# Loading a group of attention values in one transfer and sorting them with 0/1 matmuls

## The chip, the cores and the metric

The kernel runs on one core of one Trainium2 chip. The metric is the time on the device in microseconds (us), of which the median of several runs is given. A profile is one further execution, recorded by the hardware; its times count from the start of its span.

## What is computed

The reference has two parts. The first is attention over 4 batches, 8 heads, 768 positions and a head dimension of 64. Heads 0, 2 and 6 ("retrieval" heads) see every earlier key. The other five ("streaming" heads) see only the last 64 keys and the first 4 keys, the sinks.

```
scores = where(mask, q @ k.T / sqrt(64), -1e9)
a = softmax(scores)            # mask: causal for heads 0, 2, 6;
attn = a @ v                   # causal & (key < 4 | query - key < 64) for the others
x = attn as (3072, 512)
out = sum over e of p[:, e] * (relu(x @ w1[e]) @ w2[e])
```

The second part is a mixture of four dense experts over all 3072 rows: p is the normalised `domain_probs`, w1[e] is 512 x 1024 and w2[e] is 1024 x 512.

## The kernel before

The 3072 rows are worked on in eight groups of 384 rows (half of one batch each). Group g needs one attention (`attention(b, c)`) and then four expert units (`moe_steps`, one per expert). The first group's attention runs alone, at the start; the attention of group g + 1 is woven into the expert units of group g by a planner in the main loop, which counts the nanoseconds of matmuls issued. The order of the instructions of every engine is written out by hand (`manual_schedule`), and each engine executes its own list in order.

Everything that matters here happens in the first 45 us.

*Loads by SyncE and ScalarE (lines 350 to 372).* The q and k rows of group 0 come in as fp32, one load per head, with a small load `v_s32` of the four sink rows of v (line 353) between them, and then `probs`. The queue of SyncE is q1, that of ScalarE q10.

*GpSimd's list (lines 376 to 480).* GpSimd builds the masks and issues, on queue q0, all loads that turn fp32 into fp16: the values v and the expert weights. Its order before is: identity matrix, v of head 0, `mask_c`, `mask_s` (lines 397 to 420, three fills and three selects), v of heads 2, 1, 3, 4, 6, 5, w1 of expert 0 (line 300, two loads), v of head 7, w2 of expert 0 (line 306), zero fills, w1 of expert 1, a wait until w1 of expert 0 has landed (`landed`, line 460), k and q of group 1 in "triples" (line 212), w2 of expert 1, and so on.

*Where values go.* For a retrieval head, `vR` holds three tiles of 128 consecutive keys (line 269). For a streaming head, `vS` holds four tiles of 96 keys on partitions 32 to 127, and each tile also has the four sink rows on partitions 0 to 3. Before, line 275 loads the 96-key tiles from memory, and `sink_row` (line 283) copies the sink rows from `v_s32` with VectorE, once per streaming head.

*The first attention (lines 777 to 806).* For each pair of heads, `transposes` turns q and k (line 512, copies on ScalarE and VectorE); `scores(h)` multiplies (line 613), adds the mask by a matmul (line 625) and takes the exponential on ScalarE (line 631); `values(h)` multiplies with v (line 661 for retrieval heads, line 725 for streaming ones) and divides by the sum (line 678 on VectorE, or lines 743 to 758 on ScalarE). `warm_up` (line 388) adds matmuls on zeros at fixed places. The result `xT` feeds the expert units: the first layer is line 894, its relu line 907, the second layer line 918, the weighted sum on VectorE lines 930 and 934.

PSUM tiles come from three pools: pA (4 buffers), pV (2) and pO (2).

Of the kernel before, what the change touches and what calls it, by code (L numbers as in the profile page):

```python
# [9 lines left out]
FP32 = mybir.dt.float32  # L10
FP16 = mybir.dt.float16
AF = mybir.ActivationFunctionType
ALU = mybir.AluOpType
# [4 lines left out]
def kernel(  # L18
# [33 lines left out]
    nc = tc.nc  # L52
    P = 128
    B, H, S, D = q.shape
    E, DM, F = moe_w1.shape
    CH = 3 * P
# [13 lines left out]
    SH = [h for h in range(H) if not RETR[h]]  # L70
    NS = int(n_sink)
    NW = int(window)
    TK = 96
# [83 lines left out]
    def own_v(h):  # L157
        return half(PLACE[h][1])
# [10 lines left out]
    def v_tiles(b, c, h):  # L169

        if RETR[h]:
            return vR[b % 2][:, 3 * c : 3 * c + 3, RH.index(h), :]
        if b:
            return windows(vSf, c)[:, :, SH.index(h), :]
        return vS[:, c, :, SH.index(h), :]
# [89 lines left out]
    def load_v(b, c, heads):  # L265
        for h in heads:
            t = v_tiles(b, c, h)
            if RETR[h]:
                gp.dma_start(out=t[:, :, 0:D], in_=rows_of(v, b, h, c))  # L269
            elif b:  # L270
                gp.dma_start(  # L271
                    out=t[:, :, own_v(h)], in_=windows_of(v, b, h, c)
                )
            else:
                gp.dma_start(  # L275
                    out=t[R0:P, :, own_v(h)],
                    in_=tiles_of(v, b, h, c),
                )

    def sink_row(h):  # L280

        t = v_tiles(0, 0, h)
        nc.vector.tensor_copy(
            out=t[0:NS, :, own_v(h)],
            in_=v_s32[:, h : h + 1, :].to_broadcast([NS, TC, D]),
        )

    def sink_rows(b, c):
        if b:
            put_sinks(windows(vSf, c), v_sinks, c)  # L290
# [55 lines left out]

    q32 = moe.tile([P, 3, H, D], FP32, name="q32", tag="hs", bufs=2)
    k32 = moe.tile([P, 3, H, D], FP32, name="k32", tag="hs", bufs=2)

    v_s32 = pers.tile([NS, H, D], FP32, name="v_s32")  # L350
    for h in range(H):
        if h == 2:
            nc.sync.dma_start(
                out=v_s32, in_=v[0, :, 0:NS, :].rearrange("h r d -> r h d")
            )
        nc.sync.dma_start(out=k32[:, :, h, :], in_=rows_of(k, 0, h, 0))
        if h == HP:

            nc.scalar.add_instruction(
                mybir.InstLoadActFuncSet(  # L360
                    name=nc.get_next_instruction_name(),
                    engine=ENG.Activation,
                    act_func_set_id=[x.name for x in SETS].index(
                        "natural_log_exp_and_others"
                    ),
                )
            )
        eng = nc.scalar if h < HP else nc.sync
        eng.dma_start(out=q32[:, :, h, :], in_=rows_of(q, 0, h, 0))
# [5 lines left out]
    nc.vector.memset(ones, ONES)  # L375
    make_identity(nc, ident32)
    one_values(nc.vector, 0)
    load_v(0, 0, [0])
    zero(nc.vector, kR[0][:, 0, :, :, :])
    zero(nc.vector, kS[:, 0, :, :, :].rearrange("p t s x -> p s t x"))  # L380
    nc.vector.tensor_copy(out=ident16, in_=ident32)
# [13 lines left out]
    def mask_c(x, keep, drop):  # L395

        gp.memset(x, keep)
        for i in range(2):
            gp.affine_select(
                out=x[:, i * P : (i + 1) * P], in_=x[:, i * P : (i + 1) * P],  # L400
                compare_op=ALU.is_ge, fill=drop, base=0, pattern=[[1, P]],
                channel_multiplier=-1,
            )

    def mask_s(x, n, keep, drop):

        gp.memset(x, keep)
        gp.affine_select(
            out=x, in_=x, compare_op=ALU.is_ge, fill=drop,
            base=R0, pattern=[[0, n], [1, TQ]], channel_multiplier=-1,  # L410
        )
        gp.affine_select(  # L412
            out=x, in_=x, compare_op=ALU.is_ge, fill=drop,
            base=NW - 1 - R0, pattern=[[0, n], [-1, TQ]], channel_multiplier=1,
        )
        gp.memset(x[0:R0, :, :], drop)
        gp.memset(x[0:NS, :, 0:TK], keep)
        gp.affine_select(
            out=x[0:NS, 0, 0:TK], in_=x[0:NS, 0, 0:TK], compare_op=ALU.is_ge,
            fill=drop, base=-NW, pattern=[[1, TK]], channel_multiplier=-1,  # L420
        )

    def mask_w():
# [19 lines left out]
            base=WQ - 1 - NW, pattern=[[1, WQ]], channel_multiplier=-1,  # L443
        )

    mask_c(bC, 0.0, -60000.0)
    mask_s(bS[:, 0:2, :], 2, 0.0, -60000.0)
    load_v(0, 0, [2, 1, 3, 4, 6, 5])
    load_w1(0, 0, F)
    load_v(0, 0, [7])  # L450
    load_w2(0)
    zero(gp, kR[0][:, 1, :, :, :])
    zero(gp, kS[:, 1, :, :, :].rearrange("p t s x -> p s t x"))
# [40 lines left out]
    def attention(b, c):  # L494
# [109 lines left out]
        def scores(h):  # L604
            hp = h // 2
            es_of[h] = []
            for cols, parts, masks in score_tiles(h):
                ps = bank()
                if first and not es_of[h]:
                    warm_up(ps, {0: 5, 2: 8}.get(h, 0), P)  # L610
                ns = 0
                for n, (t, o, q0, nq) in enumerate(parts):
                    nc.tensor.matmul(  # L613
                        out=ps[:, o : o + nq],
                        lhsT=key_tile(b, c, h, t),
                        rhs=qTs[b, c][:, hp, q0 : q0 + nq],
                        start=(n == 0 or not first),
                        stop=not first,
                        skip_group_check=first,
                    )  # L620
                    ns += mm_ns(nq)
                if first:
                    for m, mo, o0, o1 in masks:
                        bias = bC if m is mC else bSf
                        nc.tensor.matmul(
                            out=ps[:, o0:o1], lhsT=ident16,
                            rhs=bias[:, mo : mo + o1 - o0],
                            start=False, stop=True, skip_group_check=True,
                        )
                es = att.tile([P, 512], FP16, name="es", bufs=12)  # L630
                nc.scalar.activation(  # L631
                    out=es[:, 0:cols], in_=ps[:, 0:cols], func=AF.Exp, scale=SC
                )
                for m, mo, o0, o1 in () if first else masks:
                    nc.vector.tensor_tensor(  # L635
                        out=es[:, o0:o1],
                        in0=es[:, o0:o1],
                        in1=m[:, mo : mo + o1 - o0],
                        op=ALU.mult,
                    )  # L640
                es_of[h].append((es, parts))
                if first:
                    tick(LAG)
                yield ns
# [63 lines left out]
        def values(h):  # L708
# [52 lines left out]

            yield ns + (600.0 if g == 1 else 0.0)

        def both(a, bb):

            gens = [a, bb]
            while gens:
                for gg in list(gens):
                    try:
                        yield next(gg)  # L770
                    except StopIteration:
                        gens.remove(gg)
# [4 lines left out]
        if first:  # L777
            yield from transposes(0)
            yield from scores(0)
            sink_row(1)  # L780
            sink_row(3)
            nc.scalar.copy(out=bS[:, 2, :], in_=bS[:, 1, :])
            yield from transposes(1)
            yield from scores(2)
            sink_row(4)
            sink_row(5)
            sink_row(7)
            yield from both(scores(1), values(0))
            yield from transposes(2)
            yield from both(scores(3), values(2))  # L790
            x_transposes(0)
            yield from scores(4)
            yield from transposes(3)
            yield from values(1)
            yield from both(scores(5), values(3))
            yield from both(scores(6), values(4))
            yield from both(scores(7), values(6))
            yield from values(5)
            x_transposes(6)
            yield from values(7)  # L800
            tick(LAG)
            small_things()
        else:
            sink_rows(b, c)
            order = (0, 2, 6, 1, 3, 5, 7, 4) if by_dma else (0, 2, 1, 3, 6, 5, 7, 4)
            if not by_dma:
                yield from transposes(0)
                yield from transposes(1)

            waiting = []  # L810
            for n, h in enumerate(order):
                v_steps = iter(())
                if len(waiting) > (0 if by_dma else 1):
                    v_steps = values(waiting.pop(0))
                yield from both(scores(h), v_steps)
                waiting.append(h)
                if not by_dma and n in (1, 3):
                    yield from transposes({1: 3, 3: 2}[n])
            for h in waiting:
                yield from values(h)  # L820
# [214 lines left out]
```

The softmax here doesn't subtract the row's maximum and nothing guards it: scores larger than these inputs give would overflow.

## Time and profile before

| | |
|---|---|
| median of 3 runs | 399.17 us (399.09 to 400.34) |
| span of the profiled execution | 398.9 us |
| TensorE busy | 389.1 us (98%) |
| VectorE, ScalarE, GpSimd busy | 156.6, 219.0, 143.6 us |
| first attention on TensorE | 4.69 to 20.62 us |
| loads of v of group 0 on GpSimd | eight, of 0.68 to 0.90 us each, at 1.50 to 12.28 us |

"Busy" is time in which the engine had an instruction running. A high share says that an engine is rarely idle, but not which stage is limited by what; for this one reads the timeline (instructions in order of time, with what ended the idle time before each) and the stage table (the busy time of every engine in a stretch, with TensorE's granted clock). For a load, the profile gives the time at which the engine issued it, the packets of each queue in a stretch, and the share of the 16 DMA engines' time that these took; packets overlap, so shares can exceed 100%.

### The profile page before, as it was taken

How to read it: one execution, taken by the hardware profiler on the slowest of the kernel's cores; microseconds unless marked ns; L12 is line 12 of the kernel's file. 1: busy time of each engine (PE TensorE's matmuls, PEld its weight loads, DVE VectorE, ACT ScalarE, POOL GpSimd, SP SyncE). 2: the span in 40 equal slices, each digit the busy share in tenths (PEclk: the TensorE clock that was granted, in tenths of full speed). 3: DMA queues.
4: the chain of work that ended last, by engine and by line, in shares of the span. 5: the costliest groups of instructions: out<-in, count | busy, mean ns of one | idle time of the engine just before them, and what ended most of it. 6: DMA issues, size and time to landing. Idle time of an engine off the chain costs nothing.

```text
span 398.9 us, 7125 instructions
## 1 busy us (share of the span) xinstructions
PE 389.1 (98%) x2823; PEld 220.5 (55%) x2823; DVE 156.6 (39%) x344; ACT 219.0 (55%) x468; POOL 143.6 (36%) x183
## 2 busy tenths in 40 slices
PE   7897999999999999999999999999999999999996
PEld 4753466555555555555555555555555555655553
DVE  7743585324342334433342233433443223432222
ACT  4754459535776546655664446845464456853331
POOL 8823795808907905920049101950000000000000
PEclk9999899999999999999999999999999999999999
DMA  9999999999999999990789949990472000020002
GB/s 170 154 202 204 185 196 157 130 197 136 111 196 148 113 127 130 127 120 3 126 104 163 74 80 135 97 168 12 76 123 80 5 12 0 12 79 2 0 2 80
DMA packets 166133, 42.23 MB, mean 106 GB/s; under 512 B 156396, under 2 KB 161108, under 8 KB 166100
## 3 DMA queue, kind: packets, MB, share of 16 engines
q0 software_dynamic: 102656, 20.98, 63.4%
q1 hardware_dynamic: 61700, 20.34, 26.7%
q10 hardware_dynamic: 1744, 0.46, 0.5%
q8 instruction: 22, 0.36, 0.4%
q14 instruction: 11, 0.09, 0.1%
HBM read 43.57 MB, written 6.29 MB: 125 GB/s over the span
## 4 chain that ended last, share of the span: by engine, by line
PE 89%; DMA 7%; POOL 3%; issue 0%; DVE 0%; DVEq 0%; POOLq 0%
PE pO L918 40%; PE pA L894 39%; PE pA L613 5%; DMA w2sb<-in_moe_w_dram 5%; DMA w1sb<-in_moe_w_dram 2%; PE pV L725 2%; PE pV L661 2%; POOL vS L275 1%; POOL vR L269 1%; POOL bS L412 0%; PE pV L862 0%; PE pA L515 0%; POOL k L212 0%; POOL q L212 0%; PE pV L515 0%
## 5 line engine op out<-in xcount | busy, mean ns | idle before, releaser
L894 PE MATMUL pA<-xT,w1sb 128*128 128x384 f16 x1024 | 185.9, 326 | 0.1
L918 PE MATMUL pO<-w2sb,hs 128*128 128x512 f16 x760 | 180.4, 381 | 2.8 <-DMA w2sb<-in_moe_w_dram 2.8
L907 ACT ACTIVATE hs<-pA 128x384 f16<-128x384 f32 x256 | 122.0, 492 | 94.9 <-PE pA L894 89.7
L894 PEld LDWEIGHTS <-w1sb 128*128 128x128 f16 x1024 | 95.9, 98 | 59.6 <-issue 0.5
L918 PEld LDWEIGHTS <-hs 128*128 128x128 f16 x760 | 71.0, 98 | 76.9 <-DMA w2sb<-in_moe_w_dram 3.1
L631 ACT ACTIVATE es<-pA 128x384 f16<-128x384 f32 (+2 forms) x122 | 60.0, 511 | 57.0 <-PE pA L613 55.9
L934 DVE SCALAR_TENSOR_TENSOR acc<-pO,p_sb,acc 128x512 f32<-128x512 f32 x71 | 53.3, 750 | 71.7 <-PE pO L918 71.3
L227 POOL DMA_DIRECT2D kSr<-in_k_dram x30 | 30.1, 1003 | 31.9 <-DMA kS<-kSr 21.8
L223 POOL DMA_DIRECT2D kRr<-in_k_dram x18 | 14.0, 777 | 70.8 <-DMA kR<-kRr 70.8
L748 DVE TENSOR_TENSOR xT<-pV,rc 64x384 f16<-64x384 f32 x37 | 20.5, 554 | 32.0 <-ACT rc L753 24.3
L271 POOL DMA_DIRECT2D vS<-in_v_dram x30 | 30.2, 1011 | 0.0
L930 DVE TENSOR_SCALAR acc<-pO,p_sb 128x512 f32<-128x512 f32 x24 | 18.0, 751 | 28.7 <-PE pO L918 28.5
L635 DVE TENSOR_TENSOR es<-es,mC 128x256 f16<-128x256 f16 (+1 forms) x42 | 10.9, 259 | 46.6 <-ACT es L631 45.6
L743 ACT ACTIVATE rc<-pV,eps 64x384 f32<-64x384 f32 x37 | 21.3, 576 | 12.0 <-PE pV L725 11.5
L613 PE MATMUL pA<-qT,kR 128*128 128x384 f16 (+2 forms) x120 | 24.4, 278 | 0.9 <-ACT qT L524 0.4
L753 ACT ACTIVATE rc<-rc 64x384 f32<-64x384 f32 x38 | 19.8, 521 | 1.2
L269 POOL DMA_DIRECT2D vR<-in_v_dram x24 | 19.0, 793 | 0.1
L635 DVE TENSOR_TENSOR es<-es,mW 128x384 f16<-128x384 f16 x30 | 10.7, 358 | 16.9 <-ACT es L631 16.8
L613 PEld LDWEIGHTS <-kR 128*128 128x128 f16 x120 | 11.4, 98 | 10.6 <-DVE kR L531 1.1
L661 PEld LDWEIGHTS <-es 128*128 128x128 f16 x252 | 13.2, 97 | 7.2 <-ACT es L631 0.9
L613 PEld LDWEIGHTS <-kS 128*128 128x128 f16 x255 | 13.3, 98 | 6.6
L725 PEld LDWEIGHTS <-vS 128*128 128x128 f16 x255 | 13.4, 98 | 5.9 <-DMA vS<-in_v_dram 0.4
(102 smaller groups left out, 187.6 us busy)
## 6 DMA issues: line engine op xcount, KB each, us to landing
out_dram<-acc SPq DMA_DIRECT2D x23, 256.0 KB
w1sb<-in_moe_w_dram POOLq DMA_DIRECT2D x8, 512.0 KB, 9.6
w2sb<-in_moe_w_dram POOLq DMA_DIRECT2D x4, 1024.0 KB, 14.8
kSr<-in_k_dram POOLq DMA_DIRECT2D x30, 112.0 KB, 3.8
vS<-in_v_dram POOLq DMA_DIRECT2D x30, 112.0 KB, 6.0
q<-in_q_dram POOLq DMA_DIRECT2D x18, 128.0 KB, 4.3
vR<-in_v_dram POOLq DMA_DIRECT2D x24, 48.0 KB, 5.3
kRr<-in_k_dram POOLq DMA_DIRECT2D x18, 48.0 KB, 4.2
```

Of the source, the lines that this page charges most:

```text
L227: gp.dma_start(out=kSr[:, :, SH.index(h), own(h)], in_=windows_of(k, b, h, c),)
L269: gp.dma_start(out=t[:, :, 0:D], in_=rows_of(v, b, h, c))
L271: gp.dma_start(out=t[:, :, own_v(h)], in_=windows_of(v, b, h, c))
L613: nc.tensor.matmul(out=ps[:, o : o + nq], lhsT=key_tile(b, c, h, t), rhs=qTs[b, c][:, hp, q0 : q0 + nq], start=(n == 0 or not first), stop ...
L631: nc.scalar.activation(out=es[:, 0:cols], in_=ps[:, 0:cols], func=AF.Exp, scale=SC)
L635: nc.vector.tensor_tensor(out=es[:, o0:o1], in0=es[:, o0:o1], in1=m[:, mo : mo + o1 - o0], op=ALU.mult,)
L725: nc.tensor.matmul(out=ps[:, q0 : q0 + nq], lhsT=v_tile(b, c, h, t), rhs=es[:, o : o + nq], start=(n == 0), stop=(n == len(work) - 1), ski ...
L743: nc.scalar.activation(out=rc[r, :], in_=ps[o, 0:CH], func=AF.Ln, bias=eps[o, :])
L894: nc.tensor.matmul(out=pss[ft][:, 0:CH], lhsT=w1sb[:, e * DMP + ct, ft * P : (ft + 1) * P], rhs=xT[g][:, ct, :], start=(n == 0), stop=(n = ...
L907: nc.scalar.activation(out=hs[:, ft, :], in_=ps[:, 0:CH], func=AF.Relu)
L918: nc.tensor.matmul(out=ps_o, lhsT=hs[:, ft, j * P : (j + 1) * P], rhs=w2sb[:, e * FTP + ft, :], start=(ft == 0), stop=(ft == FTP - 1),)
L934: nc.vector.scalar_tensor_tensor(out=acc[nt], in0=ps_o, scalar=p_ap, in1=acc[nt], op0=ALU.mult, op1=ALU.add,)
```

## The change

The eight loads of v of group 0 and the load of the sink rows go. In their place, one load (`load_triples`, as for k and q of group 1) puts three consecutive rows of each head on each partition of a tile `v16` (128 x 8 heads x 3 rows x 64, fp16). GpSimd issues it inside `mask_s`, after the second select. It also builds two 0/1 matrices, `pick_r` (128 x 386) and `pick_s` (128 x 4 x 3 x 128): a fill and one select for the first, ahead of `mask_s`; a fill and eight selects for the second, between the loads of w1 and w2 of expert 0.

Matmuls with slices of these matrices carry the rows from `v16` to the partitions that the tiles want, sinks included: 18 matmuls for the retrieval heads (`pick_values_r`, two PSUM tiles) and 12 for each of the sets (1, 3), (4, 5) and (7) (`pick_values_s`). ScalarE copies the five PSUM tiles into `vR` and `vS`. The calls stand at fixed places in the first attention; the five `sink_row` copies on VectorE go.

```diff
-    def sink_row(h):
...
-        if h == 2:
-            nc.sync.dma_start(
-                out=v_s32, in_=v[0, :, 0:NS, :].rearrange("h r d -> r h d")
-            )
...
-    load_v(0, 0, [0])
...
+        between()
         gp.memset(x[0:R0, :, :], drop)
...
+    pick_r = pers.tile([P, CH + 2], FP16, name="pick_r")
+    pick_s = pers.tile([P, TC, 3, P], FP16, name="pick_s")
+    def ones_where(x, base, pattern):
+        gp.affine_select(
+            out=x, in_=x, compare_op=ALU.not_equal, fill=1.0, base=base,
+            pattern=pattern, channel_multiplier=3,
+        )
     mask_c(bC, 0.0, -60000.0)
-    mask_s(bS[:, 0:2, :], 2, 0.0, -60000.0)
-    load_v(0, 0, [2, 1, 3, 4, 6, 5])
+    gp.memset(pick_r, 0.0)
+    ones_where(pick_r, 2, [[-1, CH + 2]])
+    v16 = att.tile([P, H, 3, D], FP16, name="q16", bufs=2)
+    mask_s(
+        bS[:, 0:2, :], 2, 0.0, -60000.0, lambda: load_triples(v, v16, 0, 0)
+    )
     load_w1(0, 0, F)
-    load_v(0, 0, [7])
+    gp.memset(pick_s, 0.0)
+    for t in range(TC):
+        ones_where(pick_s[:, t, :, R0:P], -TK * t, [[1, 3], [-1, TK]])
+        ones_where(pick_s[:, t, :, 0:NS], 0, [[1, 3], [-1, NS]])
     load_w2(0)
...
+        def pick_values_r(blocks, copy):
...
+            for n, t in enumerate(blocks):
+                for j in range(3):
+                    lhsT = pick_r[:, 2 + P * t - j : 2 + P * t - j + P]
+                    for h0, h1, rhs in (
+                        (0, 2, v16[:, 0:3:2, j, :]), (2, 3, v16[:, 6:7, j, :])
+                    ):
+                        nc.tensor.matmul(
...
+            copy(
+                out=vR[0][:, blocks[0] : blocks[-1] + 1, :, 0:D], in_=x
+            )
+        def pick_values_s(heads, step, copy):
...
+            for t in range(TC):
+                for j in range(3):
+                    nc.tensor.matmul(
+                        out=x[:, :, t, :], lhsT=pick_s[:, t, j, :],
+                        rhs=v16[:, heads[0] : heads[-1] + 1 : step, j, :],
...
             yield from scores(0)
-            sink_row(1)
-            sink_row(3)
             nc.scalar.copy(out=bS[:, 2, :], in_=bS[:, 1, :])
             yield from transposes(1)
             yield from scores(2)
-            sink_row(4)
-            sink_row(5)
-            sink_row(7)
+            pick_values_r([0, 1], nc.scalar.copy)
+            pick_values_r([2], nc.scalar.copy)
             yield from both(scores(1), values(0))
             yield from transposes(2)
+            pick_values_s((1, 3), 2, nc.scalar.copy)
             yield from both(scores(3), values(2))
             x_transposes(0)
             yield from scores(4)
             yield from transposes(3)
             yield from values(1)
+            pick_values_s((4, 5), 1, nc.scalar.copy)
             yield from both(scores(5), values(3))
+            pick_values_s((7,), 1, nc.scalar.copy)
             yield from both(scores(6), values(4))
```

More of the change, by code (lines that the diff above doesn't have):

```diff
@@ L278, in load_v @@
                 )
-    def sink_row(h):
[L282 to L285, printed above, removed]
-        )
     def sink_rows(b, c):
@@ L348 @@
     k32 = moe.tile([P, 3, H, D], FP32, name="k32", tag="hs", bufs=2)
-    v_s32 = pers.tile([NS, H, D], FP32, name="v_s32")
     for h in range(H):
-        if h == 2:
-            nc.sync.dma_start(
-                out=v_s32, in_=v[0, :, 0:NS, :].rearrange("h r d -> r h d")
-            )
         nc.sync.dma_start(out=k32[:, :, h, :], in_=rows_of(k, 0, h, 0))
@@ L403, in mask_c, with mask_s @@
             )
-    def mask_s(x, n, keep, drop):
+    def mask_s(x, n, keep, drop, between):
         gp.memset(x, keep)
@@ L762, in values @@
             yield ns + (600.0 if g == 1 else 0.0)
+        def pick_values_r(blocks, copy):
+            ps = pV.tile([P, 512], FP32, name="pV", bufs=2)
+            x = ps[:, 0 : len(blocks) * NR * D].rearrange(
+                "p (t h d) -> p t h d", t=len(blocks), h=NR
+            )
[6 more added lines that the diff above has]
+                        nc.tensor.matmul(
+                            out=x[:, n, h0:h1, :], lhsT=lhsT, rhs=rhs,
+                            start=(n == 0 and j == 0 and h0 == 0),
+                            stop=(n == len(blocks) - 1 and j == 2 and h0 == 2),
+                            skip_group_check=True,
+                        )
+            copy(
+                out=vR[0][:, blocks[0] : blocks[-1] + 1, :, 0:D], in_=x
+            )
+        def pick_values_s(heads, step, copy):
+            n = len(heads)
+            ps = pO.tile([P, 512], FP32, name="pO", bufs=2)
+            x = ps[:, 0 : n * TC * D].rearrange("p (s t d) -> p s t d", s=n, t=TC)
+            for t in range(TC):
[3 more added lines that the diff above has]
+                        rhs=v16[:, heads[0] : heads[-1] + 1 : step, j, :],
+                        start=(t == 0 and j == 0),
+                        stop=(t == TC - 1 and j == 2),
+                        skip_group_check=True,
+                    )
+            s0 = SH.index(heads[0])
+            copy(
+                out=vS[:, 0, :, s0 : s0 + n, own_v(heads[0])].rearrange(
+                    "p t s d -> p s t d"
+                ),
+                in_=x,
+            )
         def both(a, bb):
```

## The prediction

> **What bounds the kernel now.** I read the page first, then TensorE's stages, its timeline, and the timelines of ScalarE and GpSimd up to 42 us. On the page TensorE is busy in 98% of the span, but its clock digit drops once, in the fifth slice (40 to 50 us), and the DMA row is full to 180 us:
>
> ```profile
> PEclk9999899999999999999999999999999999999999
> DMA  9999999999999999990789949990472000020002
> ```
>
> TensorE's timeline shows where it stood still before that (start, us, instruction, wait before it):
>
> ```profile
> 20.62 5.76 PE L894 MATMUL pA<-xT,w1sb 128*128 128x384 f16 x32
> ...
> 36.26 1.47 PE L894 MATMUL pA<-xT,w1sb 128*128 128x384 f16 x8
> 40.49 1.04 PE L918 MATMUL pO<-w2sb,hs 128*128 128x512 f16 x4 [2.75 <-DMA w2sb<-in_moe_w_dram]
> ```
>
> The expert layers start at 20.62. The second expert's w2 is needed at 37.74 and starts work at 40.49: 2.75 us lost to a transfer. The stage table (length, then each engine's busy us, clock, DMA share, GB/s) shows the second half of that price:
>
> ```profile
> 37.74:40.49 2.75, 0.00 (x0) 0.00 (x1) 0.33 (x1) 0.69 (x2) 1.25 (x2) 1.00 1.20 213
> 40.49:41.58 1.09, 1.09 (x8) 0.43 (x10) 0.00 (x0) 0.00 (x0) 0.70 (x2) 1.00 1.09 205
> 41.58:45.00 3.42, 3.42 (x19) 1.39 (x18) 2.99 (x4) 0.00 (x0) 2.44 (x4) 0.51 1.47 188
> ```
>
> After the idle stretch TensorE runs 3.42 us at half clock, so another 1.7 us are lost. From 40.5 to 385 us it is busy in every stage to the last hundredth and waits for nothing. So the end is set by TensorE alone: whatever moves its work after 40.5 us moves the end by as much. What counts is (a) when the first attention ends, now 20.62, and (b) whether the 2.75 + 1.7 = 4.45 us remain.
>
> In the first attention TensorE and ScalarE hand work to each other:
>
> ```profile
> 9.14 0.30 PE L613 MATMUL pA<-qT,kS 128*128 128x160 f16 x2
> 9.42 0.35 PE L661 MATMUL pV<-vR,es 128*128 128x65 f16 x6
> 10.54 0.30 PE L613 MATMUL pA<-qT,kS 128*128 128x160 f16 x2
> 17.81 0.30 PE L661 MATMUL pV<-vR,es 128*128 128x65 f16 x4 [0.77 <-ACT es L631]
> ```
>
> ```profile
> 11.01 0.79 ACT L631 ACTIVATE es<-pA 128x320 f16<-128x320 f32 x2 [0.36 <-PE pA L625]
> 12.11 0.71 ACT L631 ACTIVATE es<-pA 128x320 f16<-128x320 f32 x2 [0.31 <-PE pA L625]
> 13.24 0.58 ACT L743 ACTIVATE rc<-pV,eps 64x384 f32<-64x384 f32 x1 [0.41 <-PE pV L725]
> 18.36 0.38 ACT L631 ACTIVATE es<-pA 128x256 f16<-128x256 f32 x1 [0.28 <-PE pA L625]
> ```
>
> To 13.24 us ScalarE waits for TensorE (0.36, 0.31, 0.41); from there to 18.1 it has no gap, and TensorE waits for it (0.77). The attention's slack is small, and the change puts work on both.
>
> **What the Trainium skill says.** "TensorE: Matmul & The Clock Gate", Part 1: the clock falls to half after an idle window and comes back after a busy one; windows run freely, 3413 ns each. The trace agrees: half clock lasts 3.42 us, and a window with 1.09 us of work in 3.41 was enough to lose it. "DMA: Bandwidth & Descriptors", "Why small descriptors are slow": each packet carries a fixed overhead. The trace agrees: alone between 7 and 8 us, q1 moved 833 packets of 256 bytes, and between 32 and 33 us q0 moved 505 packets of the three-row kind (768 bytes read):
>
> ```profile
> q1 hardware_dynamic: 833, 0.20, 112.6%
> q0 software_dynamic: 505, 0.19, 160.0%
> ```
>
> That is 19.2 and 31.7 ns of one of 16 engines. The same page, "Queues, rings and completion order": an engine serves its queues in turn, a packet at a time. The trace agrees roughly: from 8 to 9 us q1 got 511 and q0 323 packets.
>
> **Transfers.** Removed: eight loads (3072 packets, 3072 x 19.2 / 16 = 3.7 us of all engines); added: one of 1024 (x 31.7 / 16 = 2.0 us). The weights behind it gain some 1.6 us. Dropping the small sink load on SP (0.43 us of issue) lets later q and k loads start earlier; TensorE waited for none of them (no gap at 6.85), so 0.
>
> **GpSimd.** The rows that place the load:
>
> ```profile
> 1.50 0.90 POOL L269 DMA_DIRECT2D vR<-in_v_dram  x1
> 4.27 1.44 POOL L412 TENSOR_SCALAR_AFFINE_SELECT bS<-bS 128x320 f16<-128x320 f16 x1
> 6.72 0.78 POOL L269 DMA_DIRECT2D vR<-in_v_dram  x1
> 20.31 0.90 POOL L212 DMA_DIRECT2D k<-in_k_dram  x1
> ```
>
> The first load (0.90) goes; the fill of pick_r (386 columns, near the 320 and 495 columns at 0.36 and 0.54: 0.42) and its select (between 0.46 and 0.69: 0.55), with gaps 1.07, come in. So L412 ends at 5.71 - 0.9 + 1.07 = about 5.8 and the load is issued there (0.9 us, as for k). L412's 1.44 is odd: L408, the same shape, takes 0.46; without its delay the issue is at 4.8. Then 0.97 of mask, w1 at 7.7 (before 11.07; two DMAs, 1.25), the fill of pick_s (1536 columns at about 1 ns: 1.5), four selects of 288 columns (0.45 + 0.07 gap) and four of 12 (0.18 + 0.07): 3.1. pick_s is complete at 13.6, and w2 of expert 0 is issued there (before 12.95). In all this queue loses 6.0 us of issues (0.90, 0.78, 2.13, 0.75, 0.70, 0.71) and gains 6.6 (0.9, 1.07, 1.5, 3.1), so the zero fills end and w1 of expert 1 is issued some 0.7 later than before, at 18.1. The wait for w1 of expert 0, which held k, q and the second w2 until 20.07, should be over by then (it goes out 3.4 earlier), so these go out at 19.4, about 0.9 earlier. With the 1.6 us, the second w2 lands at 39 to 39.7 instead of 40.44.
>
> **TensorE's new wait.** Its order is fixed: after the scores of head 2 it reaches the first pick matmul at 9.42 - 0.28 = 9.14 and needs all of v16. Every earlier q0 load sent its first packets 1.6 to 1.9 us after its issue began: 5.8 + 1.6 = 7.4. Then each engine moves 64 packets of 31.7 ns (2.0 us) in turn with the rest of q and k: half as much again, 3.0 us, to 10.4. Landing came about 0.6 after the last packet: **11.0**. Bounds: 10.0 (L412 short), 12.3 (starved by the 16-byte packets of probs, as q0 was from 10 to 11 us with 241 packets). The wait is 1.9 us (0.9 to 3.2), with scores 1, all later matmuls, and through them every exponential queued behind it.
>
> **The pick work** (54 ns for a 128-column matmul: 12 at L515 take 0.65; about 30 for 65 columns):
> - Heads 0, 2, 6: 18 matmuls 0.75, hand-over 0.25, ScalarE copies of 384 and 192 columns 0.42 + 0.28 less overlap: values of head 0 begin 1.5 us after the landing instead of 0.28 after 9.14: **+1.2**.
> - Heads 1, 3: 12 matmuls **+0.65**, TensorE setting the pace there. pick_s (13.6) is ready as TensorE gets there (11.0 + 2.7 = 13.7): no wait, but a floor if v16 comes early. The copy runs under the next scores.
> - Heads 4, 5: the copy of 512 columns on the gapless ScalarE (exponentials of 512 take 0.60, back to back nearer 0.53): **+0.55**; the 0.65 of matmuls beside it.
> - Head 7: 256 columns: **+0.35**.
> - The five sink copies on VectorE (0.28 to 0.40) go: VectorE had gaps of 0.4 to 1.8 us, 0. The last load came late for head 7 (weight load waited 0.4): **-0.1**.
>
> Sum: 1.9 + 1.2 + 0.65 + 0.55 + 0.35 - 0.1 = **4.55 us** later into the experts. The second w2 is then needed at 37.74 + 4.55 = 42.3 and has landed: no idle, no half clock, -4.45. Net **+0.1 us**: 398.9 -> 399.0. The three timed runs lie at 399.09, 399.17 and 400.34, so on the median: **399.3**.
>
> **Rivals.**
> 1. Slower: the 1.9 us wait falls into one clock window and costs TensorE its clock inside the attention. For: with the windows of this trace (edges at 41.58 less multiples of 3.41, so 7.46 and 10.88) the one up to 10.88 holds about 0.95 us of matmuls, less than the 1.09 that lost it later. Against: the phase may differ, and ScalarE shares the path. Half clock from 10.88 to 14.29 costs TensorE half of the time after the landing: 3.3 / 2 = 1.6, plus later landing. 399.3 + 1.6 = **400.9**; it decides once a window holds under about a third of matmuls, that is from a wait of some 2 us.
> 2. Faster: L412 is short in the new order. Load, pick_s and landing come 1 us earlier, and turn-taking is kinder by half a us: 399.3 - 1.5 = **397.8**. Against: pick_s and the copies stay, so the delay hardly falls under 3 us.
> 3. The change doesn't clear the weight wait: more selects or slower ones on GpSimd delay k, q and w2 by over 3 us: the second w2 lands after 42.3 and each us beyond is paid; at 44.2 that is 399.3 + 1.9 = **401.2**. Against: by the sums above there are 2.6 us to spare.
>
> **How the numbers follow.** The cancelling case 0.42, rival 1 0.28, rival 2 0.25, rival 3 0.05. 0.3% is 1.2 us, what a measurement can tell from no change; rivals 1 and 2 lie just beyond it, so I count 7 in 10 of each past it, 8 in 10 of rival 3, and of the cancelling case, whose landing alone spans 2.3 us, 15 in 100 on each side. Faster 0.175 + 0.063 = 0.24, slower 0.196 + 0.04 + 0.063 = 0.30, same 0.46. Range: down to a landing at 10.0 with slack absorbed (397.2), up to a landing at 12.3 with half clock (401.8).
>
> **What would show it.** No wait for w2sb near 42 us and no half clock after it; a wait for v_dram before the first pick matmul at 9.1, ending near 11; the first L894 near 25.2; the v load issued near 5.8; a dip of the clock before 15 us would be rival 1. Wrong if TensorE doesn't stand at 9.1, if w2sb still ends a wait, or if the attention grows by under 3 us.

## The result

The changed kernel takes 402.99 us (median of 4 runs, 402.48 to 403.62) against 399.30 us (399.09 to 400.34, 4 runs). The ratio is 1.0088, with a 95% interval of 1.0065 to 1.0111: slower by 3.7 us, where 399.3 was forecast and the range ended at 401.8. The profiled executions are only 1.9 us apart (spans of 398.9 and 400.8 us); why the runs show twice that is the main finding below.

On the page of the changed kernel, the clock's dip is in the second slice (10 to 20 us) and no longer in the fifth (each digit is the granted clock of a slice, 9 for 90% or more):

```profile
PEclk9899999999999999999999999999999999999999
DMA  9999999999999979990689949990372000020002
```

TensorE's timeline after (start, us, instruction, wait before it) has the new wait, and the old one is gone:

```profile
9.13 0.22 PE L630 MATMUL pA<-bC,ident 128*128 128x128 f16 x1
12.21 1.59 PE L781 MATMUL pV<-q,pick_r 128*128 128x128 f16 x18 [2.87 <-DMA q<-in_v_dram]
...
32.67 5.34 PE L967 MATMUL pO<-w2sb,hs 128*128 128x512 f16 x24
...
42.53 1.47 PE L943 MATMUL pA<-xT,w1sb 128*128 128x384 f16 x8
43.84 1.03 PE L967 MATMUL pO<-w2sb,hs 128*128 128x512 f16 x4
45.26 1.90 PE L967 MATMUL pO<-w2sb,hs 128*128 128x512 f16 x8
```

TensorE stands at 9.35 until v16 (it appears as "q" here, since it shares that buffer's name) has landed at 12.2. The second expert's w2 is taken up at 43.84 without any wait, and eight of its matmuls take 1.90 us at full clock. The stage table after (length, busy us of TensorE, its weight loads, VectorE, ScalarE and GpSimd, clock, DMA share, GB/s):

```profile
9.35:11.53 2.18, 0.00 (x0) 0.00 (x0) 0.00 (x0) 0.74 (x2) 2.11 (x6) 1.00 1.43 192
11.53:14.94 3.41, 2.73 (x31) 2.61 (x31) 0.20 (x2) 1.23 (x3) 3.41 (x8) 0.51 1.37 189
14.94:26.83 11.89, 10.83 (x142) 9.72 (x141) 7.80 (x22) 9.19 (x21) 6.08 (x11) 1.00 1.31 207
```

The empty stretch costs TensorE its clock for the 3.41 us that follow, now in the attention. One wait for a load, with its half clock, was traded for another. In the kernel before, the experts' second layer started at:

```profile
26.21 5.34 PE L918 MATMUL pO<-w2sb,hs 128*128 128x512 f16 x24
```

GpSimd's timeline after has the load near where it was forecast (5.65 against 5.8), pick_s complete at 12.7, and k and the second w2 issued earlier than before (18.74 for k, before 20.31):

```profile
4.12 1.58 POOL L397 TENSOR_SCALAR_AFFINE_SELECT bS<-bS 128x320 f16<-128x320 f16 x1
5.65 1.01 POOL L212 DMA_DIRECT2D q<-in_v_dram  x1
...
10.36 2.32 POOL L439 TENSOR_SCALAR_AFFINE_SELECT pick_s<-pick_s 128x288 f16<-128x288 f16 x8
...
18.74 0.89 POOL L212 DMA_DIRECT2D k<-in_k_dram  x1
```

ScalarE's timeline after shows who stood behind TensorE: its copies waited 3.27 us for the first picks, and again 0.95 us for those of heads 1 and 3. The copies for heads 4 and 5 and for head 7 follow without a gap, as forecast for the former:

```profile
13.36 0.80 ACT L787 CAST vR<-pV 128x384 f16<-128x384 f32 x2 [3.27 <-PE pV L781]
...
16.47 0.58 ACT L806 CAST vS<-pO 128x512 f16<-128x512 f32 x1 [0.95 <-PE pO L798]
...
20.09 0.58 ACT L806 CAST vS<-pO 128x512 f16<-128x512 f32 x1
...
21.92 0.37 ACT L806 CAST vS<-pO 128x256 f16<-128x256 f32 x1
```

So the experts' second layer starts 32.67 - 26.21 = 6.46 us later. In exchange 2.75 + 1.7 = 4.45 us are gone between these two executions, net 2.0, about what their spans show (1.9).

### The profile page after: what moved, and what is told of

Its sections match the earlier page's. It is cut to its first block, busy times and chain, and to the rows that moved or that the text cites. A ratio compares the mean times of both kernels' runs of the same rounds, so it can differ in the third digit from the quotient of the medians.

```text
span 400.8 us, 7242 instructions
## 1 busy us (share of the span) xinstructions
PE 390.8 (98%) x2877; PEld 223.7 (56%) x2877; DVE 154.7 (39%) x339; ACT 221.0 (55%) x473; POOL 143.2 (36%) x187
## 4 chain that ended last, share of the span: by engine, by line
PE 94%; DMA 2%; ACT 1%; POOL 1%; DVE 1%; issue 0%; DVEq 0%; POOLq 0%
PE pA L943 42%; PE pO L967 41%; PE pA L618 5%; PE pV L666 2%; PE pV L730 2%; DMA q<-in_v_dram 2%; ACT rc L748 0%; DVE xT L753 0%; PE pV L781 0%; POOL bS L397 0%; PE pA L517 0%; PE pV L911 0%; ACT es L636 0%; PE pA L520 0%; PE pV L520 0%
## 5 line engine op out<-in xcount | busy, mean ns | idle before, releaser
L748 ACT ACTIVATE rc<-pV,eps 64x384 f32<-64x384 f32 x37 | 21.3, 575 | 12.1 <-PE pV L730 11.5
L269 POOL DMA_DIRECT2D vR<-in_v_dram x21 | 16.9, 810 | 0.0
L618 PE MATMUL pA<-qT,kS 128*128 128x55 f16 (+4 forms) x255 | 16.9, 196 | 0.0
```

The costliest lines, as they stand in the source:

```text
L618: nc.tensor.matmul(out=ps[:, o : o + nq], lhsT=key_tile(b, c, h, t), rhs=qTs[b, c][:, hp, q0 : q0 + nq], start=(n == 0 or not first), stop ...
L748: nc.scalar.activation(out=rc[r, :], in_=ps[o, 0:CH], func=AF.Ln, bias=eps[o, :])
```

## Experiments

**Is it the clock, and what does it cost? (two runs)** The first fills TensorE's new wait with matmuls that compute nothing, the second the old wait in the kernel before.

```diff
+            fill = pV.tile([P, 512], FP32, name="pV", bufs=2)
+            warm_up(fill, 24, 256)
             pick_values_r([0, 1], nc.scalar.copy)
```

> The changed kernel with 24 matmuls of 256 columns on zeros ahead of the first pick matmul (about 2.6 us at full clock, inside the 2.87 us for which TensorE waits there). They compute nothing that is used. Theory: TensorE's half clock between about 11.5 and 14.9 us follows from the empty wait and costs 1.0 to 1.4 us; with the wait filled the clock stays full and the time falls by that much, to about 401.8 us, while the landing of v16 stays at 12.2. Rival: ScalarE and the landing set the pace there, and the clock costs nothing: no change within 0.4 us.

Measured: 402.38 us (7 runs, five of them at 401.9 to 402.9 with the clock full or nearly so and two at 405.4 and 406.1 with one window lost); ratio to the kernel before 1.0085 (1.0051 to 1.0118). The median falls by 0.6 us, less than the 1.0 to 1.4 expected; in this profile v16 also landed later, at 12.87. TensorE's timeline:

```profile
9.56 2.78 PE L373 MATMUL pV<-warm 128*128 128x256 f16 x24
12.87 0.93 PE L781 MATMUL pV<-q,pick_r 128*128 128x128 f16 x18 [0.53 <-DMA q<-in_v_dram]
...
32.38 5.34 PE L969 MATMUL pO<-w2sb,hs 128*128 128x512 f16 x24
```

The same 18 pick matmuls now take 0.93 instead of 1.59 us. From their start to the experts' second layer it is 32.38 - 12.87 = 19.51 us here and 32.67 - 12.21 = 20.46 in the changed kernel: the half clock costs 0.95 us, measured so that the later landing drops out. Before, TensorE needed 26.21 - 9.14 = 17.07 us from the same point on; so 19.51 - 17.07 = 2.44 us are left for picks, copies and what they push back. The delay of 6.46 us is thus split into 3.07 (9.14 to 12.21) + 0.95 + 2.44; the three sum to it by construction, and each rests on one or two profiles.

```diff
                 ps_o = pO.tile([P, DM], FP32, name="pO", bufs=2)
+                if g == 0 and e == 1 and j == 0:
+                    warm_up(ps_o, 10, DM)
```

> The kernel before with 10 matmuls of 512 columns on zeros ahead of the second expert's first second-layer matmul, where TensorE waited 2.75 us for w2 (2.16 us at full clock). Theory: the profiled execution of the kernel before (400.69 us as timed) paid 1.7 us for a half clock after this wait that most of its runs (399.1 to 399.4) do not pay. Then the filled wait leaves the median at 399.3 within 0.4 us, and only removes the occasional slower run. Rival: every run pays the 1.7 us: the median falls to about 397.6 us. If the wait is shorter in most runs than in the profile, the fill itself costs up to 1 us.

Measured: 398.95 us (22 runs, 398.58 to 400.73, all at full clock), ratio 0.9982 (0.9969 to 0.9995). The 28 runs of the kernel before beside it, sorted by the mean clock of each:

```
clock 0.999 to 1.000   16 runs   398.80 to 399.61 us
clock 0.996            11 runs   400.49 to 401.03 us
clock 0.991             1 run    402.51 us
```

One half-clock window (3.42 us) in 399 us is 0.4% of the mean clock and 1.7 us, which is the distance of the groups. So the 1.7 us are paid by some runs and not by others, and the profile that the prediction read (clock 0.996, 400.69 us as timed) was one that paid. With the wait filled, none of the 22 does, against 12 of the 28 beside them. "TensorE: Matmul & The Clock Gate", Part 1, of the Trainium skill says that the windows run freely and do not restart with a kernel; the groups fit that, since the same wait may or may not empty one window enough. Where the windows lay in the timed runs isn't recorded, so this reason is argued; that the clock makes the two groups is shown.

**The changed kernel again, beside its variants.**

> The changed kernel as it is, on the same chip as its variants. Theory: v16 lands at 12 to 14 us and every run loses one clock window (mean clock 0.996) or two (0.99): 403 us, 2.5 to 4.5 us above the kernel before, whose runs fall into two groups, near 399.1 at full clock and near 400.8 with one window lost. Rival: the changed kernel too falls into two groups, and its faster one lies within 1 us of the faster one of the kernel before.

Measured: 403.00 us (8 runs): six with one window lost at 402.5 to 403.9, two with two lost at 404.3 and 406.1; none at full clock. In its profile the picks start at 12.14 and take 1.60 us, and the experts' second layer follows 32.74 - 12.14 = 20.60 us later, so by this one the half clock costs 1.09 us. The ratio is 1.0071 (1.0045 to 1.0097) to 52 runs of the kernel before with a median of 400.82, since more of these happened to lose a window. Its median of 399.3 or 400.8 is thus a matter of how many runs of each kind are drawn. Against its 20 full-clock runs (median 399.2), the six of the changed kernel with one window lost (median 402.7) take 3.5 us more. From the profiles one gets 6.46 - 2.75 = 3.7.

**An earlier load.** The changed kernel with v16 issued right after the identity matrix:

```diff
     one_values(nc.vector, 0)
+    v16 = att.tile([P, H, 3, D], FP16, name="q16", bufs=2)
+    load_triples(v, v16, 0, 0)
...
-    mask_s(
-        bS[:, 0:2, :], 2, 0.0, -60000.0, lambda: load_triples(v, v16, 0, 0)
-    )
+    mask_s(bS[:, 0:2, :], 2, 0.0, -60000.0, lambda: None)
```

> The changed kernel with one thing moved: the load of v16 is issued on GpSimd right after the identity matrix, ahead of all masks, where the load of head 0 stood before the change. Theory: the loss is TensorE's wait for v16 (2.87 us in the profile of the changed kernel) and the half clock that follows from it. The load then lands near 8.5 us, the wait goes, the clock stays full, the first second-layer matmul moves from 32.67 to about 29 us, and the time falls by about 4 us, to 399 us. Rival: the pick matmuls and their copies are the loss, and the wait only hides in their place: the time falls by under 1 us. A third outcome: the early load takes turns with q and k of the first heads, and TensorE starts later instead.

> The kernel with the early load of v16 once more, for a second profile, since the first profiled execution (410.15 us) was 7 us above that kernel's other runs. Theory: the eight q and k loads and v16 share the same 16 DMA engines, so an earlier v16 makes q and k of the second pair late: TensorE waits 1 to 3 us for q or k before 12 us and not for v16, and the time is again near 403 us. Rival: the waits for q and k were peculiar to that execution: none over 0.5 us here, and the attention as long as in the run with the picks later.

Measured: 403.25 us (6 runs; 403.19 without the one at 410.15; ratio 1.0088, 1.0064 to 1.0112), then 404.26 in the single run. The wait for v16 is gone and nothing is won: the third outcome. The first profiled execution (410.15 us) lies apart from the other five (402.8 to 404.3), so the lines are those of the second, TensorE's and then SyncE's:

```profile
9.34 0.52 PE L516 MATMUL pA<-ident,q 128*128 128x128 f32 x3 [2.17 <-DMA q<-in_q_dram]
...
11.34 0.93 PE L780 MATMUL pV<-q,pick_r 128*128 128x128 f16 x18
...
18.47 0.88 PE L516 MATMUL pA<-ident,q 128*128 128x128 f32 x3 [1.94 <-DMA q<-in_q_dram]
```

```profile
7.55 2.42 SPq L355 DMA_DIRECT2D q<-in_q_dram  x1
```

TensorE waits 2.17 us for q or k of the second pair and 1.94 us for those of the last. SyncE itself is held up: issuing one load of q takes it 2.42 us (in the changed kernel 0.37 to 0.49), and its last q goes out at 10.78 instead of 7.04. And v16, issued at 1.50, lands at 10.1 and not at 8.5. What v16 gains, q and k lose.

**What holds the load back on GpSimd.** The odd select of 1.44 us before the load took 1.58 after the change (line 397), and in the early-load kernel another select took 1.86 at 3.90 to 5.76. I changed the order of VectorE's fills:

```diff
-    one_values(nc.vector, 0)
     zero(nc.vector, kR[0][:, 0, :, :, :])
     zero(nc.vector, kS[:, 0, :, :, :].rearrange("p t s x -> p s t x"))
+    one_values(nc.vector, 0)
```

> The changed kernel with VectorE's first fills in another order: the zero fills of kR and kS ahead of the fills with ones. It asks why one GpSimd select takes 1.5 us where the same shape takes 0.46, just before the load of v16. Theory: GpSimd is held while VectorE fills kS (4.2 to 5.3 us); with that fill at about 2 to 3 us another GpSimd instruction is held, the select takes 0.46, the load is issued near 4.6 to 5.0 us instead of 5.65. Rival: the select is slow by itself, whatever VectorE does: it stays at 1.4 to 1.6 us and the load at 5.65.

Measured: 402.74 us (5 runs, 401.8 to 403.4; ratio 1.0056, 1.0033 to 1.0079). GpSimd's timeline, and TensorE's:

```profile
4.12 0.46 POOL L397 TENSOR_SCALAR_AFFINE_SELECT bS<-bS 128x320 f16<-128x320 f16 x1
4.52 1.01 POOL L212 DMA_DIRECT2D q<-in_v_dram  x1
```

```profile
12.69 0.93 PE L781 MATMUL pV<-q,pick_r 128*128 128x128 f16 x18 [2.78 <-DMA q<-in_v_dram]
```

The select takes 0.46 and the load goes out 1.13 us earlier, so the delay does depend on VectorE's order. That VectorE's fill of kS by itself holds GpSimd isn't shown: here that fill ran at 2.04 to 3.16 us beside a select of pick_r that took its normal 0.51. What the profiles do show is a common end: the slow selects began at 4.27 (before), 4.12 (after) and 3.89 to 3.90 (early load), and all ended at 5.70 to 5.76. They look held up until a fixed point, not slower at their work; what holds them stays open. And v16 still lands no sooner: from issue to landing it took 8.1 us here, 6.5 in the changed kernel and 8.8 in the first profile with the early load.

**Work in place of the wait.** The changed kernel with more scores ahead of the first pick matmul:

```diff
             yield from scores(2)
+            yield from scores(1)
+            yield from transposes(2)
+            yield from scores(3)
+            yield from scores(4)
             pick_values_r([0, 1], nc.scalar.copy)
             pick_values_r([2], nc.scalar.copy)
-            yield from both(scores(1), values(0))
-            yield from transposes(2)
+            yield from both(scores(5), values(0))
             pick_values_s((1, 3), 2, nc.scalar.copy)
...
```

> The changed kernel, same loads, masks, matmuls and copies, with the first attention's steps in another order: the scores of heads 1, 3, 4 and 5 and the transposes of the third pair go ahead of the first pick matmul, and the values of all heads follow. TensorE and ScalarE then have about 3 us of their own work while v16 is under way. Theory: the wait (2.87 us) and the half clock behind it are the loss, not the pick work. The first second-layer matmul moves from 32.67 to about 29 us, the clock stays full, and the time falls by 3 to 4 us from the changed kernel's 403.0, to 399.0 to 400; below the kernel before only if the copies are hidden too. Rival: the pick matmuls and copies are the loss: the attention stays long and the time stays above 401.5.

Measured: 400.49 us (22 runs, 20 of them at 399.9 to 402.5 with the clock nearly full); ratio 1.0015 (0.9997 to 1.0033). TensorE's timeline:

```profile
12.81 0.93 PE L781 MATMUL pV<-q,pick_r 128*128 128x128 f16 x18
...
24.00 0.34 PE L707 MATMUL pV<-ident,x_pair 128*128 128x128 f16 x3 [1.16 <-DVE x_pair L686]
...
30.71 5.34 PE L969 MATMUL pO<-w2sb,hs 128*128 128x512 f16 x24
```

No wait, no half clock, 2.5 us less than the changed kernel, if not the 3 to 4 expected: most of the loss was the wait with its half clock. Clock for clock it stays slower than the kernel before: its 20 runs at nearly full clock have a median of 400.35, 1.1 us above the 399.2 of that kernel's. The kernel before in the same order is the control:

> The kernel before, without the change, in the same new order of the first attention's steps. It tells apart what the order gives by itself. Theory: the second expert's w2 lands at about 40.4 us whatever the attention does, so a shorter attention only lengthens the wait for it: the time stays at 399.4 within 0.5 us. Rival: the order itself is what gains: 1 us or more below the kernel before.

Measured: 399.32 us (14 runs, 398.8 to 400.1, none with a whole window lost), ratio 0.9975 (0.9960 to 0.9990). Its timeline:

```profile
28.67 5.34 PE L920 MATMUL pO<-w2sb,hs 128*128 128x512 f16 x24
...
40.20 1.04 PE L920 MATMUL pO<-w2sb,hs 128*128 128x512 f16 x4 [0.20 <-DMA w2sb<-in_moe_w_dram]
```

Against the full-clock runs of the kernel before (median 399.2) nothing is won, as expected: w2 lands at 40.2, and a longer attention only takes up the wait, with no window lost. Between the two kernels in the same order, picks and copies cost 30.71 - 28.67 = 2.04 us.

**Which engine sets the pace?** Copies of the streaming heads on VectorE, in the changed kernel and in the one with the picks later:

```diff
-            pick_values_s((1, 3), 2, nc.scalar.copy)
+            pick_values_s((1, 3), 2, nc.vector.tensor_copy)
...
```

> The changed kernel with the three copies of the streaming heads' values (512, 512 and 256 columns) on VectorE instead of ScalarE. Theory: ScalarE has no gap from the first copy to the last exponentials, so these copies lie on the path for 0.55 + 0.35 us or a little more: the time falls by 0.5 to 1.2 us, to about 402 us. Rival: TensorE sets the pace there, or VectorE becomes late for the rows of q and k: no change within 0.4 us, or slower.

> As the run with the picks later, with the three copies of the streaming heads' values on VectorE instead of ScalarE. Theory: ScalarE then sets the pace of the first attention, so its 1.5 us of copies count: 0.5 to 1.5 us below that run. Rival: VectorE or TensorE sets the pace: no change within 0.4 us.

Measured: 403.81 us (6 runs, ratio 1.0102, 1.0073 to 1.0132) and 400.83 us (22 runs, ratio 1.0019, 1.0000 to 1.0038). Neither falls, so the theory that ScalarE alone sets the pace is refuted; whether TensorE does, or VectorE becomes late in its turn, these runs don't tell apart. In the first of them v16 landed at 13.7 us in the profile (a wait of 4.05), so its landing also moves by over a us from one execution to the next.

Then two runs that feed ScalarE further ahead, the second without the matmuls on zeros before the values:

```diff
             yield from scores(4)
+            yield from scores(5)
             pick_values_r([0, 1], nc.scalar.copy)
...
-            yield from both(scores(6), values(3))
+            yield from both(scores(7), values(3))
             pick_values_s((7,), 1, nc.scalar.copy)
-            yield from both(scores(7), values(4))
             yield from values(6)
+            yield from values(4)
```

> The changed kernel with the scores of heads 1, 3, 4 and 5 ahead of the first pick matmul, as in the earlier run with the picks later, and with the values of head 6 ahead of those of head 4, so that VectorE's last product is ready when its transposes come (TensorE waited 1.16 and 0.44 us for VectorE there). Theory: the wait for v16 stays hidden and 1 to 1.5 us of TensorE's waits go: 1 to 1.5 us below that run's 400.3, so 398.8 to 399.4, level with the kernel before. Rival: the pick work on ScalarE sets the end whatever the order: no change against that run within 0.4 us.

> The run before this one without the 26 matmuls on zeros ahead of the values of heads 3 to 7, which compute nothing. Theory: the pick matmuls now keep TensorE busy, and where TensorE sets the pace up to 2.8 us of these matmuls come off the path: the attention ends 1 to 2 us earlier, and since the second expert's w2 lands near 38.2 us in this kernel, not 40.4, the time falls below both kernels, to 397.5 to 398.5. Rival: TensorE's clock falls to half without them, or ScalarE sets the pace: no gain, or a loss of 1 us.

```diff
-                warm_up(ps, {6: 8}.get(h, 0), 256)
+                pass
...
-                warm_up(ps, {3: 4, 4: 4, 5: 6, 7: 4}.get(h, 0), 256)
+                pass
```

Measured: 401.05 us (22 runs, ratio 1.0017, 1.0003 to 1.0032) and 401.37 us (22 runs, ratio 1.0025, 1.0009 to 1.0041). Neither comes to its forecast (398.8 to 399.4 and 397.5 to 398.5). The first one's two waits for VectorE became one of another kind, again near the end:

```profile
24.77 0.61 PE L373 MATMUL pO<-warm 128*128 128x256 f16 x4 [1.69 <-DVE xT L753]
```

In the second, 7 of the 22 runs kept the full or nearly full clock and most of them took 399.5 to 399.7 us; 15 lost one window (400.8 to 401.5) or two (401.8 to 402.8). With the matmuls on zeros only one of 22 runs lost a window, so they were holding the clock. The theory was half right: the 7 runs that kept the clock (median 399.6) are 1.4 us below those of the first run that did (401.0), but most runs lost it. No version with the picks that I tried beats the kernel before at full clock (399.3 beside these two). The only two variants whose ratio to the kernel before lies below 1 with its whole interval are that kernel itself without its clock loss: 398.95 us with the filled wait and 399.32 us in the new order.

## Why the prediction was wrong

The mechanism was right: a new wait for v16 at 9.1, pick work behind it, and the wait for w2 gone. Three terms of the sum were mis-sized.

1. **The gain.** "no idle, no half clock, -4.45" came true in the profiled execution. The failed step is "Net +0.1 us: 398.9 -> 399.0 ... so on the median: 399.3". The -4.45 holds 1.7 us of half clock that only part of the runs pay. The median of 399.17 is, by its time, that of a run at full clock, so 1.7 us were taken off a time that did not hold them. The gain on the median is 2.75. This is 1.7 of the 3.6 us missed.
2. **The landing.** "Landing came about 0.6 after the last packet: 11.0" was 12.2, near the late bound of 12.3. The issue was as forecast (5.65 against 5.8), the first packets came at 7.5 to 8 (forecast 7.4), but the packets took until 11.5 instead of 10.4. The forecast priced a packet at 31.7 ns of an engine and added half for turns with q and k. Turns alone don't explain it: from 8.5 to 9.5 us q1 got 9 packets, and v16, with the engines nearly to itself, moved 356 where that price gives 505. The wait from 9.14 was 3.07 us, not 1.9: 1.2 us.
3. **The clock in the attention** was rival 1, given 0.28, and stood at nothing in the sum; its own estimate, "a wait of some 2 us", lay just above the 1.9 us forecast. Every one of the 12 runs of the changed kernel lost at least one window, and both of its profiles show it behind this wait of 3.07 us. It cost 0.95 to 1.09, not 1.6 us: 0.7 us of the slow window lay in the wait itself, and only 2.73 us of matmuls in it. The rest of the difference isn't explained by a run.
4. **Picks and copies**: 2.65 us forecast, 2.44 measured (2.04 in the other order). Right. Pick_s as a floor played no part: it was complete at 12.7, and its first matmul stood at 15.6.
5. **Transfers**: the second w2 was forecast at 39 to 39.7. GpSimd's wait for it ended at 38.3, and 42.3 was the forecast need, against 43.84 measured. GpSimd's own work was priced too long: pick_s took 1.41 for its fill and 2.32 for its selects, not 1.5 and 3.1. Rival 3 is excluded. Rival 2 asked for a short select and an earlier landing; the run with another order of fills had the first and not the second.

By terms, with the forecast first: wait 1.9 / 3.07, clock 0 / 0.95, picks 2.65 / 2.44, gain -4.45 / -2.75 on the full-clock runs; sum +0.1 / +3.7.

What would have shown it in time: the profiled execution took 400.69 us as timed while the median was 399.17. That gap of 1.5 us is nearly one half-clock window, and the profile showed just one.

What stays open: why v16 needs 4 us for its packets and lands at 12.1 to 13.7. That v16 and the loads of q and k hold each other up is shown by the early load. But from 8.5 to 9.5 us both were slow at once, and no run shows why.

## What to carry to other kernels

Removing a wait for a transfer on the busiest engine pays only if the new path adds less than that wait; here 6.46 us were added for 2.75. Merging eight loads into one also means here that no pick can start until all of it has landed. Before using the sizes of one profile, compare its own time with the median and count its half-clock windows: a term that only some executions pay must not be booked against the median. An order that puts about three us of independent instructions ahead of the first use won back 2.5 us; the two earlier issues of the load won back nothing that the runs can tell.

## What the runs showed of the hardware

- While v16's packets were served, the other loads nearly stopped, although SyncE had issued them all by 8.06 us. From 8 to 10 us, before and then after the change (queue: packets, MB, share of the 16 engines' time; q0 carries v16 after the change):

```profile
q1 hardware_dynamic: 1222, 0.29, 73.5%
q0 software_dynamic: 638, 0.08, 62.0%
```

```profile
q0 software_dynamic: 630, 0.24, 112.4%
q1 hardware_dynamic: 185, 0.04, 15.8%
```

  After the change, from 8.5 to 9 and from 9 to 9.5 us:

```profile
q0 software_dynamic: 129, 0.05, 109.2%
q1 hardware_dynamic: 4, 0.00, 0.9%
```

```profile
q0 software_dynamic: 227, 0.09, 146.9%
q1 hardware_dynamic: 5, 0.00, 1.9%
```

  "DMA: Bandwidth & Descriptors", "Issuing engines are not separate DMA queues", of the Trainium skill says that all loads run on the same 16 engines and interleave. The early load agrees that they hold each other up. The turns a packet at a time on which the prediction built aren't what this stretch shows: 356 packets against 9.
- From 17 to 20 us the small packets of `probs` (16 bytes each) went one for one with the large ones of q0 (566 of q1 and 569 of q0). Here a small packet took a turn like a large one.
- The same GpSimd select took 1.44 to 1.59 us in one order of VectorE's fills and 0.46 in another; when the early load moved GpSimd's list, another select took 1.86 instead of 0.51.
- Two stretches of 3.41 us, counted back from where the half clock began, held 1.09 us of matmuls (before, 38.17 to 41.58) and 0.83 us (after, 8.12 to 11.53). Each was followed by half clock for one stretch of the same length (3.42 and 3.41 us). How little work it takes isn't measured; of the executions of the kernel before, with the wait of 2.75 us in its profile, 12 of 28 lost the clock.
